# V as the stationary operand in a looped decode step, and 32 positions of K on TensorE in place of ScalarE's sums

## The chip, the cores and the metric

The kernel runs on one core of one Trainium2 chip. The metric is the time of one execution on the device in microseconds (us). TensorE's weight loads (PEld) and matmuls (PE), VectorE (DVE), ScalarE (ACT) and GpSimd (POOL) work beside each other; SyncE (SP) issues the large transfers. Each engine has its own list of instructions, read by its own sequencer, and engines wait for each other through semaphores. SBUF is the memory on the chip, with 128 partitions; PSUM is where TensorE writes.

## What is computed

One token for each of two batches passes through an attention block with a cache, and then through a gated MLP. The cache is what costs: 32 heads with 8192 positions of 128 numbers, for K and for V, in bf16, for two batches.

```python
def _A_ref(x, k_cache, v_cache, wq, wo):          # x: 2 x 1 x 512
    q = (x @ wq) ... 32 heads of 128
    scores = einsum("bhqd,bhkd->bhqk", q, k) * (Dh ** -0.5)
    p = softmax(scores, axis=-1)
    o = einsum("bhqk,bhkd->bhqd", p, v)
    return o ... @ wo

h = x + _A_ref(_layernorm(x), k_cache, v_cache, wq, wo)
h2 = h + _B_ref(_layernorm(h), W_gate, W_up, W_down)   # relu(gate) * up, then W_down
```

## The kernel before

The attention runs in 16 steps, `steps`, of one batch and four heads each (`H4`). A step's K is one block of 128 partitions by 256 positions (`NT`) by 128 numbers, 8 MiB; its V is another. In the block, 32 partitions (`QP`) belong to one head, so each partition holds 256 positions of one head. There are three block buffers, `buf`. K of step i goes to buffer (i-2) mod 3, and V of step i goes into the same buffer as soon as that K has been used up (`k_at`, `v_at`). So K of step i+1 can come in only when the V of step i-2 has been read.

`scores(i)` makes the 256 scores of a partition, for the positions in three ways:

- VectorE multiplies K by q in place (`mult`, L341) for `nmul` positions, 240 in most steps.
- The first 48 of these (`NACT`) are summed over their 128 numbers by ScalarE, one position at a time (`sum_up`, L348: one activation and one read of the accumulator each). The other 192 are added up by VectorE in four halving steps (L412) and one reduction (L416).
- The last 16 positions (`NPE`; 32 in the last step, none in the first) aren't multiplied: TensorE transposes them in chunks of eight (L356), ScalarE copies a chunk from PSUM to `kT` (L362), and TensorE multiplies the chunk by q (L364). ScalarE copies the results into the scores (L375).

`best(i)` takes the maximum of a partition (L312) and spreads it by a matmul (L314). `powers(i)` finds the step's maximum (L323), and ScalarE makes the four sets of exponentials into `pgz`, with their sums in `zc` (L326).

`values(i)` multiplies the exponentials with V on TensorE, in two forms. In the first 13 steps (`COLS`) the exponentials are stationary: a group of four positions (`T4`) with 16 columns is loaded as weights, and 512 numbers of V stream past, into a PSUM tile `po`. The first two groups are written out (L427); the other 62 are a loop on TensorE alone, `Fori`, with two groups a turn (`LOOP`), so 31 turns (L451 for the turn's own bookkeeping, L453 for the matmuls), whose addresses are worked out in registers from the turn's number w. A turn's records name these operations: FUSED_REGOPS and ALU_OP are register instructions, COMPARE_BRANCH ends the turn. The loop stands in a critical section: TensorE's sequencer waits for several semaphores on entry (L447, L659) and marks its end (L447). Because every head's exponentials meet every position's V there, the wanted parts are picked out later: `collect` copies `po` to `ob` (L465), and `turn` multiplies `ob` with the 0/1 pattern `sel` for a group of steps (L474) and forms the sums with `sums` (L295). In the last three steps V is stationary, 128 numbers of one position at a time, and the four columns of exponentials of that position stream past (L439), all 256 written out with fixed addresses.

The order on TensorE, VectorE, ScalarE and SyncE is the order in which the code emits it (`manual_schedule`). In a middle step it is: VectorE multiplies 16 and then 176 positions; TensorE transposes two chunks; ScalarE sums the first 16 positions and copies the last `po`; the two chunks are copied and multiplied; `powers(i-1)`; `turn(i-2)`; `values(i-1)` on TensorE; SyncE issues K of step i+1; ScalarE copies the chunks' scores, VectorE multiplies the last 48 positions, ScalarE sums 32 more; VectorE adds up, and `best(i)`. After that SyncE issues V of step i. So on TensorE the loop over V of step i-1 stands behind the transposes of K of step i, and the maximum of step i behind that loop.

Of the kernel before, what the change touches and what calls it, by code (L numbers as in the profile page):

```python
# [7 lines left out]
ACT = mybir.ActivationFunctionType  # L8
ALU = mybir.AluOpType
# [14 lines left out]
def kernel(  # L24
# [21 lines left out]
    H4 = 4  # L46
# [70 lines left out]
    ob = consts.tile([P, T4 * Dh], f32)  # L117
    ident = consts.tile([P, P], bf16)
# [5 lines left out]
    pick = consts.tile([P, B, QP], bf16)  # L124
    sel = consts.tile([P, T4, 4, H4], f32)
    eps_col = consts.tile([P, 1], f32)
# [43 lines left out]
    with tc.manual_schedule(engines=ORDERED):  # L170
# [13 lines left out]
        select(nscale, -SCALE, 0, [[-1, P]], 1)  # L184
        nc.gpsimd.memset(pgz, 0.0)
        nc.gpsimd.memset(zc, 0.0)
        nc.gpsimd.memset(ob, 0.0)

# [9 lines left out]

        nc.gpsimd.memset(sel, 0.0)
        for j in range(H4):  # L200
            select(sel[:, :, :, j], 1.0, -j, [[-H4, T4], [-32, 4]], 1)
        for k, n in enumerate(rows):
# [67 lines left out]

        groups = {3: (0, 0, 4), 7: (0, 4, 4), 11: (1, 0, 4)}
        for i in range(12, N):
            groups[i] = (1, i - NG, 1)
        assert NG == 8 and COLS == 13

        divided = {NG - 1: (0, 0, NG), N - 3: (1, 0, NG - 2), N - 2: groups[N - 2], N - 1: groups[N - 1]}
        o_ps = {}
        made = {}

        def group(i):  # L280
            e = min(k for k in groups if k >= i)
            return e, steps[i][1] - groups[e][1]

        waiting = []


        def o_of(i):
            key = B if i == N - 1 else steps[i][0]
            if key not in o_ps:
                o_ps[key] = ps2.tile([P, 2, Hq], f32, tag="o", name="o_ps")  # L290
            return o_ps[key]

        def sums(i):
            b, g0, n = groups[i]
            nc.tensor.matmul(  # L295
                out=o_of(i)[:, 1, H4 * g0:H4 * (g0 + n)], lhsT=mean_w, rhs=zc[:, b, g0:g0 + n, :], start=True, stop=True,
            )
# [21 lines left out]
        def powers(i):  # L319
            b, g = steps[i]  # L320
            scol = scols.pop(i)
            nm = small.tile([P, H4], f32, tag="nm")
            nc.vector.tensor_reduce(out=nm, in_=mx.pop(i), axis=AXIS.X, op=ALU.min)  # L323
            for j in range(H4):
                r = slice(j * QP, (j + 1) * QP)
                nc.scalar.activation(  # L326
                    out=_free(pgz[r, :], j, [[H4, NT]]), in_=scol[r, :], func=ACT.Exp, scale=SCALE,
                    bias=nm[r, j:j + 1], accum_out=zc[r, b, g, j:j + 1],
                )

        def scores(i):
# [3 lines left out]
            nmul = NT - NPE[i]  # L335
            na = NACT[i]
            scol = scols[i] = small.tile([P, NT], f32, tag=f"scol{i % 2}", name="scol")

            def mult(t0, t1):
# [3 lines left out]
                )  # L343

            def sum_up(t0, t1):
                for t in range(t0, t1):
                    whole = ps.tile([P, Dh], f32, tag="acc", name="whole")
                    nc.scalar.activation(  # L348
                        out=whole, in_=kt[:, t * Dh:(t + 1) * Dh], func=ACT.Copy, accum_out=scol[:, t:t + 1],
                    )  # L350

# [26 lines left out]
            if i == 0:  # L378
                for t0 in range(0, NT, NT // 4):
                    mult(t0, t0 + NT // 4)  # L380
                sum_up(0, na)
            elif last:
                mult(0, nmul)
                scores_of(by_columns([transposed(c0) for c0 in (0, TPC)]))
                sum_up(0, na)
# [21 lines left out]
            n = nmul - na  # L407
            width = Dh
            while width > 8:
                half = width // 2  # L410
                lo = _free(kt, na * Dh, [[Dh, n], [1, half]])
                nc.vector.tensor_tensor(  # L412
                    out=lo, in0=lo, in1=_free(kt, na * Dh + half, [[Dh, n], [1, half]]), op=ALU.add,
                )
                width = half
            nc.vector.tensor_reduce(  # L416
                out=scol[:, na:nmul], in_=_free(kt, na * Dh, [[Dh, n], [1, 8]]), axis=AXIS.X, op=ALU.add,
            )
# [4 lines left out]

        def products(i, u0, u1):
            v = buf[v_at[i]]
            for u in range(u0, u1):
                nc.tensor.matmul(  # L427
                    out=made[i][0:H4 * T4, :], lhsT=pgz[:, u * H4 * T4:(u + 1) * H4 * T4],
                    rhs=v[:, u * T4 * Dh:(u + 1) * T4 * Dh],
                    start=(u == 0), stop=(u == NT // T4 - 1), skip_group_check=True,  # L430
                )

        def values(i):
            v = buf[v_at[i]]
            if i >= COLS:
                sums(i)
                g = steps[i][1]
                for t in range(NT):
                    nc.tensor.matmul(  # L439
                        out=o_of(i)[:, 0, H4 * g:H4 * (g + 1)],  # L440
                        lhsT=v[:, t * Dh:(t + 1) * Dh], rhs=pgz[:, H4 * t:H4 * (t + 1)],
                        start=(t == 0), stop=(t == NT - 1),
                    )
                return

            made[i] = ps.tile([P, T4 * Dh], f32, tag="po", name="po")
            with tc.tile_critical(sync_engine=PE):  # L447
                products(i, 0, LOOP)

                at = {PE: LOOP_AT} if i == 0 else None  # L450
                with nc.Fori(1, NT // T4 // LOOP, 1, engines=[PE], head_slot=at) as w:  # L451
                    for u in range(LOOP):
                        nc.tensor.matmul(  # L453
                            out=made[i][0:H4 * T4, :],
                            lhsT=pgz[:, bass.ds((w * LOOP + u) * (H4 * T4), H4 * T4)],
                            rhs=v[:, bass.ds((w * LOOP + u) * (T4 * Dh), T4 * Dh)],
                            start=False, stop=True, skip_group_check=True,
                        )


        def collect(i):
            if i >= COLS:
                return
            _, k = group(i)
            nc.scalar.activation(  # L465
                out=ob[32 * k:32 * k + H4 * T4, :], in_=made.pop(i)[0:H4 * T4, :], func=ACT.Copy,
            )

        def turn(i):
            if i in groups:  # L470
                if i < COLS:
                    _, g0, n = groups[i]
                    for t in range(T4):
                        nc.tensor.matmul(  # L474
                            out=o_of(i)[:, 0, H4 * g0:H4 * (g0 + n)], lhsT=ob[:, t * Dh:(t + 1) * Dh],
                            rhs=sel[:, t, 0:n, :], start=(t == 0), stop=(t == T4 - 1),
                        )
                    sums(i)
                if i in divided:
                    waiting.append(i)  # L480

# [182 lines left out]
```

## Time and profile before

| what | before |
|---|---|
| median of three runs | 668.6 us (667.44 to 668.81) |
| the profiled execution | 667.49 us |
| its span, first to last instruction | 665.8 us |
| mean granted TensorE clock, share of full speed | 0.805 |
| VectorE busy | 507.8 us (76%) |
| ScalarE busy | 419.9 us (63%) |
| TensorE matmul busy | 366.8 us (55%) |
| read from memory | 281.05 MB |

The profile is of one execution. Its page gives the busy time of every engine, the span in 40 slices, the DMA queues, the chain of work that ended last, and the costliest groups of instructions by line of the kernel; "L453 PE" is the matmul of line 453. A q behind an engine (PEq, SPq, and PEldq in lists of a line's instructions) is its sequencer, whose instructions don't count as busy time. Times in lists are from the span's start. Rows of the list by time give start and length in us, engine, line, operation, operands, count, and in brackets how long the engine was idle before and what ended that.

### The profile page before, as it was taken

What the parts mean: (1) busy time and instruction counts of PE and PEld (TensorE: products, weight loads), DVE (VectorE), ACT (ScalarE), POOL (GpSimd) and SP (SyncE); (2) the same over time, 40 slices, a digit from 0 to 9 for tenths busy, and PEclk for the clock granted to TensorE, in tenths of its full rate; (3) what the DMA queues carried; (4) which work ended last, traced back from release to release, by engine and by line L of the source; (5) the groups of instructions that cost most, each with busy time, mean ns of one, the idle gap of its engine ahead of it and who ended that gap; (6) DMA issues with size and microseconds to landing.
All of it is one profiled execution on the core that took longest, in us unless ns stands there. A gap on an engine that the chain in (4) does not pass through costs nothing. (4 is left out here: it accounts for less than half of the span.)

```text
span 665.8 us, 10067 instructions
## 1 busy us (share of the span) xinstructions
PE 366.8 (55%) x2601; PEld 148.8 (22%) x2601; DVE 507.8 (76%) x192; ACT 419.9 (63%) x1766; POOL 8.4 (1%) x51
## 2 busy tenths in 40 slices
PE   2601574747647474664638657473865667543456
PEld 1201111111211221121112212111221131242456
DVE  0799969597795959879595996959689595987911
ACT  2596848487594848749475784848669465883720
POOL 5000000000000000000000000000000000000000
PEclk9955696988969798896978979698896979955555
DMA  8999999999999999999999999999999998999996
GB/s 369 448 441 441 434 441 406 426 437 434 441 437 438 434 433 418 433 434 434 437 438 429 425 426 429 423 409 437 426 433 418 425 407 367 429 443 439 414 416 260
DMA packets 6933, 281.45 MB, mean 423 GB/s; under 512 B 786, under 2 KB 884, under 8 KB 1524
## 3 DMA queue, kind: packets, MB, share of 16 engines
q1 hardware_dynamic: 6896, 281.06, 98.5%
q8 instruction: 15, 0.25, 0.1%
q14 instruction: 18, 0.15, 0.1%
q10 hardware_dynamic: 4, 0.00, 0.0%
HBM read 281.05 MB, written 0.00 MB: 422 GB/s over the span
## 5 line engine op out<-in xcount | busy, mean ns | idle before, releaser
L341 DVE TENSOR_TENSOR buf<-buf,qrep 128x2048 bf16<-128x2048 bf16 (+4 forms) x47 | 262.0, 5600 | 104.2 <-DMA buf<-in_A_k_cache_dram 104.2
L453 PE MATMUL po<-buf,pgz 128*16 x806 | 264.7, 408 | 87.8 <-issue 87.6
L348 ACT ACTIVATE whole<-buf 128x128 f32<-128x128 bf16 x752 | 211.4, 281 | 145.3 <-DVE buf L341 122.4
L412 DVE TENSOR_TENSOR buf<-buf 128x12288 bf16<-128x12288 bf16 (+3 forms) x64 | 203.1, 3173 | 2.2
L348 ACT ACTIVATION_READ_ACCUMULATOR whole<-buf 128x1 f32 x752 | 140.2, 186 | 0.2
L453 PEld LDWEIGHTS po<-buf,pgz 128*16 x806 | 72.5, 90 | 285.1 <-issue 241.6
L326 ACT ACTIVATE pgz<-scol,nm 32x256 bf16<-32x256 f32 x64 | 55.0, 859 | 14.0 <-DVE nm L323 10.4
L427 PE MATMUL po<-buf,pgz 128*16 128x512 bf16 x26 | 13.3, 614 | 85.4 <-ACT whole L348 83.0
L362 ACT ACTIVATE kT<-t_ps 128x1024 bf16<-128x1024 bf16 x32 | 32.8, 1024 | 18.9 <-PE t_ps L356 9.7
L439 PE MATMUL o_ps<-pgz,buf 128*128 128x4 bf16 x768 | 21.6, 166 | 20.5 <-DMA buf<-in_A_v_cache_dram 14.6
L364 PE MATMUL sc_ps<-qT,kT 128*128 128x4 bf16 x256 | 11.5, 167 | 38.1 <-ACT kT L362 38.1
L416 DVE TENSOR_REDUCE scol<-buf 128x192 f32<-128x1536 bf16 (+1 forms) x16 | 28.2, 1761 | 0.6
L314 PE MATMUL mx_ps<-nscale,pm 128*128 128x128 f32 x32 | 8.3, 345 | 34.0 <-DVE pm L312 29.3
L439 PEld LDWEIGHTS <-buf 128*128 128x128 bf16 x768 | 21.2, 104 | 21.0 <-DMA buf<-in_A_v_cache_dram 14.8
L356 PE MATMUL t_ps<-ident,buf 128*128 128x128 bf16 x256 | 19.6, 236 | 5.9 <-DMA buf<-in_A_k_cache_dram 5.9
L427 PEld LDWEIGHTS po<-buf,pgz 128*16 128x16 bf16 x26 | 1.3, 90 | 86.5 <-issue 86.5
L465 ACT ACTIVATE ob<-po 16x512 f32<-16x512 f32 x13 | 7.6, 587 | 18.2 <-PEq L447 18.2
L356 PEld LDWEIGHTS <-buf 128*128 128x128 bf16 x256 | 17.7, 107 | 6.4 <-DMA buf<-in_A_k_cache_dram 6.2
L364 PEld LDWEIGHTS <-kT 128*128 128x128 bf16 x256 | 8.7, 98 | 42.7 <-ACT kT L362 42.7
L326 ACT ACTIVATION_READ_ACCUMULATOR pgz<-scol,nm 32x1 f32 x64 | 15.9, 249 | 0.0
L314 PEld LDWEIGHTS mx_ps<-nscale,pm 128*128 128x128 f32 x32 | 5.4, 210 | 38.0 <-issue 28.3
L312 DVE TENSOR_REDUCE pm<-scol 128x1 f32<-128x256 f32 x16 | 6.7, 420 | 8.7 <-ACT whole L348 8.4
(88 smaller groups left out, 103.1 us busy)
## 6 DMA issues: line engine op xcount, KB each, us to landing
buf<-in_A_k_cache_dram SPq DMA_DIRECT2D x4, 2048.0 KB, 23.7
buf<-in_A_v_cache_dram SPq DMA_DIRECT2D x2, 4096.0 KB, 41.1
buf<-in_A_wq_dram SPq DMA_DIRECT2D x1, 4096.0 KB, 12.6
buf<-in_A_wo_dram SPq DMA_DIRECT2D x1, 2048.0 KB, 14.6
buf<-in_A_wo_dram SPq DMA_DIRECT2D x2, 1024.0 KB, 18.7
buf<-in_B_W_gate_dram SPq DMA_DIRECT2D x1, 1376.0 KB
buf<-in_B_W_up_dram SPq DMA_DIRECT2D x1, 1376.0 KB, 24.5
buf<-in_B_W_down_dram SPq DMA_DIRECT2D x1, 768.0 KB, 25.9
```

The costliest lines, as they stand in the source:

```text
L314: nc.tensor.matmul(out=mx[i].rearrange("p a b -> p (a b)"), lhsT=_free(pm, 0, [[0, P]]), rhs=nscale, start=True, stop=True,)
L326: nc.scalar.activation(out=_free(pgz[r, :], j, [[H4, NT]]), in_=scol[r, :], func=ACT.Exp, scale=SCALE, bias=nm[r, j:j + 1], accum_out=zc[r ...
L341: nc.vector.tensor_tensor(out=kv, in0=kv, in1=_free(qrep[b], g * Dh, [[0, t1 - t0], [1, Dh]]), op=ALU.mult,)
L348: nc.scalar.activation(out=whole, in_=kt[:, t * Dh:(t + 1) * Dh], func=ACT.Copy, accum_out=scol[:, t:t + 1],)
L356: nc.tensor.transpose(t_ps[:, k, :], kt[:, t * Dh:(t + 1) * Dh], ident)
L362: nc.scalar.activation(out=kT, in_=t_ps.pop(0).rearrange("p t s -> p (t s)"), func=ACT.Copy)
L364: nc.tensor.matmul(out=sc_ps[:, c0 + t, :], lhsT=kT[:, t * P:(t + 1) * P], rhs=_free(qT, H4 * g * B + b, [[B, H4]]), start=True, stop=True,)
L412: nc.vector.tensor_tensor(out=lo, in0=lo, in1=_free(kt, na * Dh + half, [[Dh, n], [1, half]]), op=ALU.add,)
L416: nc.vector.tensor_reduce(out=scol[:, na:nmul], in_=_free(kt, na * Dh, [[Dh, n], [1, 8]]), axis=AXIS.X, op=ALU.add,)
L427: nc.tensor.matmul(out=made[i][0:H4 * T4, :], lhsT=pgz[:, u * H4 * T4:(u + 1) * H4 * T4], rhs=v[:, u * T4 * Dh:(u + 1) * T4 * Dh], start=( ...
L439: nc.tensor.matmul(out=o_of(i)[:, 0, H4 * g:H4 * (g + 1)], lhsT=v[:, t * Dh:(t + 1) * Dh], rhs=pgz[:, H4 * t:H4 * (t + 1)], start=(t == 0) ...
L453: nc.tensor.matmul(out=made[i][0:H4 * T4, :], lhsT=pgz[:, bass.ds((w * LOOP + u) * (H4 * T4), H4 * T4)], rhs=v[:, bass.ds((w * LOOP + u) * ...
```

## The change

The 13 looped steps take V as the stationary operand too: the same form as the last three steps, one position at a time, 128 numbers of V loaded as weights and four columns of exponentials streaming past. Eight positions (`LOOP = 8`) are written out, and the other 248 are a loop of 31 turns with eight positions each, whose addresses come from registers. The results go straight to the step's columns of `o_ps`, so `po`, `ob`, `sel`, `collect`, `made`, `groups` and the matmuls with `sel` go, and `sums(i)` stands at the head of each `values(i)`.

On the K side `sum_up` goes. VectorE adds up all that it multiplies. TensorE takes 32 positions (24 in the first step, 48 in the second, 40 in the last), so VectorE multiplies and adds 224, in pieces of 176 and 48 where it was 16, 176 and 48. `pgz` has two buffers, for even and odd steps. In step 1 `powers(0)` stands ahead of the first multiplication.

```diff
-    FIRST = 16
     MIDDLE = 176
-    T4 = 4
...
-    LOOP = 2
+    LOOP = 8
...
-    pgz = consts.tile([P, NT * H4], bf16)
+    pgz = [consts.tile([P, NT * H4], bf16, name=f"pgz{s}") for s in range(2)]
...
-    NACT = {i: 32 if i == N - 1 else 48 for i in range(N)}
-    NPE = {i: 0 if i == 0 else 32 if i == N - 1 else 16 for i in range(N)}
+    NPE = {i: (24, 48)[i] if i < 2 else 40 if i == N - 1 else 32 for i in range(N)}
...
             else:
-                mult(0, FIRST)
                 if i == 1:
                     powers(i - 1)
-                mult(FIRST, FIRST + MIDDLE)
+                mult(0, MIDDLE)
                 t_ps = [transposed(c0) for c0 in (0, TPC)]
-                sum_up(0, FIRST)
-                if i >= 2:
-                    collect(i - 2)
                 sc_ps = by_columns(t_ps)
...
-                mult(FIRST + MIDDLE, nmul)
-                sum_up(FIRST, na)
+                mult(MIDDLE, nmul)
...
         def values(i):
+            b, g = steps[i]
             v = buf[v_at[i]]
+            p = pgz[i % 2]
+            o = o_of(i)[:, 0, H4 * g:H4 * (g + 1)]
+            sums(i)
+
+            def products(n):
+                for t in range(n):
+                    nc.tensor.matmul(
+                        out=o, lhsT=v[:, t * Dh:(t + 1) * Dh], rhs=p[:, H4 * t:H4 * (t + 1)],
+                        start=(t == 0), stop=(t == NT - 1), skip_group_check=True,
+                    )
+
             if i >= COLS:
-                sums(i)
...
+                products(NT)
                 return
 
-            made[i] = ps.tile([P, T4 * Dh], f32, tag="po", name="po")
             with tc.tile_critical(sync_engine=PE):
-                products(i, 0, LOOP)
+                products(LOOP)
 
                 at = {PE: LOOP_AT} if i == 0 else None
-                with nc.Fori(1, NT // T4 // LOOP, 1, engines=[PE], head_slot=at) as w:
+                with nc.Fori(1, NT // LOOP, 1, engines=[PE], head_slot=at) as w:
+                    vw = v[:, bass.ds(w * (LOOP * Dh), LOOP * Dh)]
+                    pw = p[:, bass.ds(w * (LOOP * H4), LOOP * H4)]
                     for u in range(LOOP):
                         nc.tensor.matmul(
-                            out=made[i][0:H4 * T4, :],
-                            lhsT=pgz[:, bass.ds((w * LOOP + u) * (H4 * T4), H4 * T4)],
-                            rhs=v[:, bass.ds((w * LOOP + u) * (T4 * Dh), T4 * Dh)],
+                            out=o, lhsT=vw[:, u * Dh:(u + 1) * Dh], rhs=pw[:, u * H4:(u + 1) * H4],
                             start=False, stop=True, skip_group_check=True,
                         )
```

More of the change, by code (lines that the diff above doesn't have):

```diff
@@ L114 @@
     qrep = [consts.tile([P, NG, Dh], bf16, name=f"qrep{b}") for b in range(B)]
-    pgz = consts.tile([P, NT * H4], bf16)
+    pgz = [consts.tile([P, NT * H4], bf16, name=f"pgz{s}") for s in range(2)]
     zc = consts.tile([P, B, NG, H4], f32)
-    ob = consts.tile([P, T4 * Dh], f32)
     ident = consts.tile([P, P], bf16)
@@ L124 @@
     pick = consts.tile([P, B, QP], bf16)
-    sel = consts.tile([P, T4, 4, H4], f32)
     eps_col = consts.tile([P, 1], f32)
@@ L184 @@
         select(nscale, -SCALE, 0, [[-1, P]], 1)
-        nc.gpsimd.memset(pgz, 0.0)
+        for t in pgz:
+            nc.gpsimd.memset(t, 0.0)
         nc.gpsimd.memset(zc, 0.0)
-        nc.gpsimd.memset(ob, 0.0)
         nc.gpsimd.memset(fold, 0.0)
@@ L197 @@
         select(quarter, 0.0, P // KC - 1, [[P // KC, KC]], -1, ALU.is_ge)
-        nc.gpsimd.memset(sel, 0.0)
-        for j in range(H4):
-            select(sel[:, :, :, j], 1.0, -j, [[-H4, T4], [-32, 4]], 1)
         for k, n in enumerate(rows):
@@ L268 @@
         nc.scalar.activation(out=qT, in_=qT_ps, func=ACT.Copy)
-        groups = {3: (0, 0, 4), 7: (0, 4, 4), 11: (1, 0, 4)}
-        for i in range(12, N):
-            groups[i] = (1, i - NG, 1)
         assert NG == 8 and COLS == 13
-        divided = {NG - 1: (0, 0, NG), N - 3: (1, 0, NG - 2), N - 2: groups[N - 2], N - 1: groups[N - 1]}
+        divided = {NG - 1: (0, 0, NG), N - 3: (1, 0, NG - 2), N - 2: (1, NG - 2, 1), N - 1: (1, NG - 1, 1)}
         o_ps = {}
[L278 to L282, printed above, removed]
         waiting = []
@@ L293, in sums @@
         def sums(i):
-            b, g0, n = groups[i]
+            b, g = steps[i]
             nc.tensor.matmul(
-                out=o_of(i)[:, 1, H4 * g0:H4 * (g0 + n)], lhsT=mean_w, rhs=zc[:, b, g0:g0 + n, :], start=True, stop=True,
+                out=o_of(i)[:, 1, H4 * g:H4 * (g + 1)], lhsT=mean_w, rhs=zc[:, b, g, :], start=True, stop=True,
             )
@@ L326, in powers @@
                 nc.scalar.activation(
-                    out=_free(pgz[r, :], j, [[H4, NT]]), in_=scol[r, :], func=ACT.Exp, scale=SCALE,
+                    out=_free(pgz[i % 2][r, :], j, [[H4, NT]]), in_=scol[r, :], func=ACT.Exp, scale=SCALE,
                     bias=nm[r, j:j + 1], accum_out=zc[r, b, g, j:j + 1],
@@ L335, in scores @@
             nmul = NT - NPE[i]
-            na = NACT[i]
             scol = scols[i] = small.tile([P, NT], f32, tag=f"scol{i % 2}", name="scol")
@@ L343, in mult @@
                 )
[L345 to L350, printed above, removed]
             def transposed(c0):
@@ L379, in scores @@
                 for t0 in range(0, NT, NT // 4):
-                    mult(t0, t0 + NT // 4)
-                sum_up(0, na)
+                    mult(t0, min(t0 + NT // 4, nmul))
+                scores_of(by_columns([transposed(c0) for c0 in (0, TPC)]))
             elif last:
@@ L410, in scores @@
                 half = width // 2
-                lo = _free(kt, na * Dh, [[Dh, n], [1, half]])
+                lo = _free(kt, 0, [[Dh, nmul], [1, half]])
                 nc.vector.tensor_tensor(
-                    out=lo, in0=lo, in1=_free(kt, na * Dh + half, [[Dh, n], [1, half]]), op=ALU.add,
+                    out=lo, in0=lo, in1=_free(kt, half, [[Dh, nmul], [1, half]]), op=ALU.add,
                 )
@@ L416, in scores @@
             nc.vector.tensor_reduce(
-                out=scol[:, na:nmul], in_=_free(kt, na * Dh, [[Dh, n], [1, 8]]), axis=AXIS.X, op=ALU.add,
+                out=scol[:, 0:nmul], in_=_free(kt, 0, [[Dh, nmul], [1, 8]]), axis=AXIS.X, op=ALU.add,
             )
@@ L422, in scores, with values @@
             best(i)
-        def products(i, u0, u1):
+        def values(i):
+            b, g = steps[i]
             v = buf[v_at[i]]
[L426 to L434, printed above, removed]
-            if i >= COLS:
-                sums(i)
[L437 to L443, printed above, removed]
+            p = pgz[i % 2]
[7 more added lines that the diff above has]
+                    )
+            if i >= COLS:
+                products(NT)
@@ L452, in values @@
                     for u in range(LOOP):
                         nc.tensor.matmul(
-                            out=made[i][0:H4 * T4, :],
-                            lhsT=pgz[:, bass.ds((w * LOOP + u) * (H4 * T4), H4 * T4)],
-                            rhs=v[:, bass.ds((w * LOOP + u) * (T4 * Dh), T4 * Dh)],
+                            out=o, lhsT=vw[:, u * Dh:(u + 1) * Dh], rhs=pw[:, u * H4:(u + 1) * H4],
                             start=False, stop=True, skip_group_check=True,
                         )
[L461 to L467, printed above, removed]
@@ L469, in turn @@
-        def turn(i):
[L470 to L480, printed above, removed]
+        def turn(i):
+            if i in divided:
+                waiting.append(i)
```

2 lines of the change are left out of this document (removed).

## The prediction

> **What bounds the kernel now.** I read the page's slices and queues first, then what the DMA queue itself waits for, then its issues in order of time.
>
> ```profile
> span 665.8 us, 10067 instructions
> DMA  8999999999999999999999999999999998999996
> q1 hardware_dynamic: 6896, 281.06, 98.5%
> SPq L145 <- DVE scol L416: 330.8, 15, 31.1
> SPq L145 <- PEq L447: 216.1, 13, 20.8
> 280.02 0.33 SPq L145 DMA_DIRECT2D buf<-in_A_v_cache_dram  x1
> 287.90 13.03 DVE L341 TENSOR_TENSOR buf<-buf,qrep 128x2048 bf16<-128x2048 bf16 x2 [7.46 <-DMA buf<-in_A_k_cache_dram]
> 297.39 0.33 SPq L145 DMA_DIRECT2D buf<-in_A_k_cache_dram  x1
> ```
>
> The DMA row is full in nearly every slice, and the queue that carries K and V is busy 98.5% of the span: the kernel streams 281 MB and the engines keep up. SP issues a V when VectorE has reduced the K that lies in its buffer (L416), and a K when the loop over V has left its block (L447). The last three rows show how early. A V is issued at 280.02 while the K ahead of it lands at 287.9; the next K is issued at 297.39, and that V lands only at 307.9, when TensorE's wait ahead of its loop ends. So both issues come 8 to 10 us before the queue would run dry. The issues of K from 101.83 to 493.77 are ten steps apart: 39.2 us a step, the time of 16.8 MB.
>
> How near is TensorE to that? Its own chain of a step is the loop over V, then the maximum (L314), the transposes of the next K, copy and matmul by ScalarE and TensorE in turn, the four exponentials, and the loop again. In the step from 537 to 573 that chain ran without a wait for a transfer: last turn at 537.22, first static matmul of the next loop at 545.73, last turn at 573.07, so 35.9 us. Spare: about 3 us of 39.2. This is the row to watch.
>
> **The loop, which decides.** These are the instructions of the present loop, sequencer's own included (count: shortest/median/longest ns):
>
> ```profile
> L451 PEldq FUSED_REGOPS  x403: 78/78/83, 74.2 to 572.5; - x135
> L451 PEldq ALU_OP  x403: 32/32/32, 74.7 to 573.0; - x135
> L451 PEldq COMPARE_BRANCH  x404: 76/208/225, 73.9 to 573.1; - x135
> L453 PEldq FUSED_REGOPS  x806: 42/58/79, 74.3 to 572.7; - x162
> L453 PEldq ALU_OP  x403: 36/36/42, 74.6 to 572.9; - x135
> 583.54 4.03 PE L439 MATMUL o_ps<-pgz,buf 128*128 128x4 bf16 x145 [1.94 <-DMA buf<-in_A_v_cache_dram]
> ```
>
> 403 turns are 13 loops of 31. A turn has two matmuls, and for them five register instructions and a branch: fused 78, fused 42, [load, matmul], fused 74, ALU 36, [load, matmul], ALU 32, branch 208. In the trace the next one starts 58 to 61 ns after the end of the one before, and 78 to 81 where a load and a matmul stand between. Sum: 78+59+42+78+74+59+36+81+32+61+208+58 = 866 ns. From branch to branch the loops turn every 884 to 890 ns (one loop, from 505.5 on, every 1034): 27.4 us for 31 turns. So the loop is paced by TensorE's sequencer; its two matmuls fill 0.63 us of a turn.
>
> The last row is the V-stationary form with fixed addresses: 145 pairs in 4.03 us, 27.8 ns each. The data of the new form is nearly free, but only while no register instruction stands between two pairs.
>
> The changed loop has eight positions a turn, so sixteen addresses that change with w. The product with w is shared, then every position adds its own constant to both. I take one fused instruction of 74 ns per position after the first, for this reason: the second position of today's turn (sum, products, both bases) needs 74 and 36, and a shared product removes about what the 36 did. Turn: first position 78+59+36+80 = 253, seven more of 74+79 = 1071, the end 32+61+208+58 = 359: 1683 ns. 31 turns: **52.2 us**, for 27.4 now. Bounds: the shortest fused row, 42, gives 1459 ns and 45.2 us; two register instructions per position (74+59+36+80 = 249 each) give 2355 ns and 73.0 us. I take 74 because this row adds for two addresses, as the new positions must.
>
> [...]
>
> **The rest of TensorE's chain**, from a loop's end to the next loop's first turn. End to transposes 0.8 (573.15 to 573.98), and 0.3 for a slower clock, since the array will be idle for most of the loop. Step 15 already has four chunks of eight positions, at that clock:
>
> ```profile
> 602.89 1.89 PE L356 MATMUL t_ps<-ident,buf 128*128 128x128 bf16 x16 [5.86 <-DMA buf<-in_A_k_cache_dram]
> 608.89 1.02 ACT L362 ACTIVATE kT<-t_ps 128x1024 bf16<-128x1024 bf16 x1 [0.52 <-PE sc_ps L364]
> 544.46 0.25 ACT L326 ACTIVATION_READ_ACCUMULATOR pgz<-scol,nm 32x1 f32 x1
> 545.73 0.59 PE L427 MATMUL po<-buf,pgz 128*16 128x512 bf16 x1 [2.34 <-PEq L447]
> ```
>
> Transposes to the end of the fourth copy: 602.89 to 609.91, 7.0 us (two chunks took 3.2). Four exponentials 3.5. Their end to the first static matmul, 544.71 to 545.73, 1.0: the critical section's waits; the new sums(i) lies beside it. Eight static pairs and the first register move 0.3. Together 12.9. The second pgz buys nothing: the exponentials stand behind the four copies on ScalarE, and these wait for transposes that stand behind the loop. So a step of TensorE takes 52.2+12.9 = **65.1 us against 39.2 for its transfers**: TensorE becomes the bound, by 26 us a step.
>
> **What else changes, and why it costs nothing then.** ScalarE loses 48 sums a step, 48 times 0.43 = 21 us, and one collect of 0.59, and gets two copies of 1.02; it waited 122 us for VectorE. VectorE multiplies 224 for 240 positions (16.5 to 15.2 us) and adds 224 for 192 (12.7 to 14.9, and the reduction 1.75 to 2.04): 1.2 us more, 32 of 65. Without the longer loop this would go into its wait of 104.2 us for K, 6 to 7 a step. The products with sel and their groups go (L474, 4.5 us in all). GpSimd's fills lie in the first 9 us. K i+1 and V i are issued as before, after the loop and after L416, by SP in the same order, with nothing moved past another; both land far ahead of need.
>
> **The sum.** First turn 74.2 as now, since V 0 lands at 72.7 either way: 74.3. Twelve steps of 65.1 and one loop of 52.2: loop 12 ends at 907.7 (573.15 now). Then K 15 goes out; V 14 waits for VectorE: 1.6 to the new minimum, 3.35 multiply, 14.9 adds, 2.0 reduction, so issue 22.0 later and landing 22 after that on an empty queue: 951.7. From V 14's landing on, the tail is today's: 622.9 to 665.8, 42.9. Span 994.6. One loop of thirteen now pays 150 ns more a turn in a gap between two instructions; a body of 27 instructions for 11 makes such a place likelier, so two loops at 4.7: 1004. The execution is 667.49 for a span of 665.8, so 1.7 more: **1006 us**. That execution stands 0.2% below the median of 668.6.
>
> **Rivals.**
> - *One register step for the turn, none per position* (not slower). Turn 253+7x21+359 = 759 ns, loop 23.5, step 36.4, under 39.2: the transfers stay the bound and the time is today's, 667 to 669, or a little less where ScalarE's sums ended last (8.4 us of VectorE's waits). It decides from a loop of 26.3 us, 850 ns a turn. For it: 27.8 ns a pair with fixed addresses. Against it: every pair of L453 has register instructions of its own today. [...]
> - *Cheaper addresses*, 42 ns: step 58.1, end 905 (74.3+697.2+45.2+86.9+1.7).
> - *Two instructions per position*: step 85.9, end 1267.
> - *The change not doing what it says*: the diff gives 32 positions to thirteen of the steps and 24, 48 and 40 at the ends; that moves 3 us at most.
>
> **How the numbers follow.** Forecast 0.75, cheaper addresses 0.08, two instructions 0.08, not slower 0.05, something else slower (fetch gaps in most loops, 31x0.15x13 = 60 us more) 0.04. The forecast's own terms, a turn of 1.65 to 1.80 us, 12 to 14.5 around it, up to four loops with a gap, give 970 to 1085. With the cheaper addresses the range is 900 to 1090. A measurement here can tell 0.2% from no change: faster 0.02, same 0.03, slower 0.95.
>
> **What would show it.** Right: L447's waits gone from TensorE's entry, SP waiting for PEq at almost every K, DMA near 6 tenths, turns of about 1.7 us with seven fused instructions of 74 more, steps of 65 us. Wrong: a turn under 0.85 us, or fewer register instructions than positions.

## The result and the profile after

The changed kernel takes **1017.1 us**, the median of three runs (1016.94 to 1021.14), against 668.6 before: 1.524 times as long, with a 95% interval of 1.519 to 1.529. Its profiled execution has a span of 1015.2 us, where the prediction's sum came to 1004, and a mean granted TensorE clock of 0.518.

The first lines are from its page: the span, the granted clock and the DMA share in 40 slices, and the queue that carries K and V.

```profile
span 1015.2 us, 16654 instructions
...
PEclk9555555555555555555555555555555555555555
DMA  9999296492771945909649268194590960954998
...
q1 hardware_dynamic: 6896, 281.06, 65.9%
```

The same 281.06 MB move, but the DMA row is no longer full. It swings between 0 and 9, because transfers now come in bursts with pauses between them. What SP waits for before it issues one (us in all, times, the longest) says who makes the pauses:

```profile
SPq L140 <- PEq L409: 581.4, 13, 52.0
SPq L140 <- DVE scol L383: 326.5, 15, 31.1
```

The 13 waits for the end of TensorE's critical section (L447 before, L409 now) have grown from 216.1 to 581.4 us. VectorE's part of the waits has not grown (330.8 before). Next the waits of ScalarE and VectorE, and of the array itself:

```profile
ACT kT L336 <- PE t_ps L330: 744.8, 14, 63.7
DVE nm L305 <- PE mx_ps L296: 420.5, 16, 39.4
PEld o_ps L417 <- issue: 205.2, 409, 0.9
...
DVE buf L322 <- DMA buf<-in_A_k_cache_dram: 27.7, 15, 5.9
...
PE mx_ps L296 <- PEq L409: 5.3, 13, 0.4
```

ScalarE and VectorE wait for TensorE, and hardly for data any more (27.7 us, where VectorE waited 104.2 for K). TensorE itself waits for "issue", which is time in which the engine waited for nothing that the profile shows: its own sequencer had not reached the next instruction. This is the loop by its instructions (count: shortest/median/longest ns, first and last start), in two lists, one for the line of the matmuls and one for the turn's bookkeeping:

```profile
L417 PEld LDWEIGHTS o_ps<-pgz,buf x3224: 101/104/106, 74.4 to 927.0; 128*128 x190
L417 PE MATMUL o_ps<-pgz,buf x3224: 164/184/188, 74.4 to 927.0; 128*128 x190
L417 PEldq FUSED_REGOPS  x2821: 74/74/74, 74.5 to 926.8; - x189
L417 PEldq ALU_OP  x403: 36/36/42, 74.3 to 925.8; - x135
```

```profile
L413 PEldq COMPARE_BRANCH  x404: 76/208/222, 74.0 to 927.1; - x135
L413 PEldq FUSED_REGOPS  x403: 78/78/83, 74.2 to 925.7; - x135
L413 PEldq ALU_OP  x403: 32/32/32, 75.6 to 927.0; - x135
```

3224 pairs of load and matmul are 403 turns of eight. Their 2821 fused instructions are seven a turn, one for every position after the first, and each lasts 74 ns. From branch to branch a turn takes 1.70 us (before: 0.884 for the same share of V). One step of TensorE in order of time, from the last turns of a loop to the second turn of the next:

```profile
455.85 0.97 PE L417 MATMUL o_ps<-pgz,buf 128*128 x6
457.21 0.76 PE L296 MATMUL mx_ps<-nscale,pm 128*128 128x128 f32 x2 [0.39 <-PEq L409]
457.76 1.91 PE L330 MATMUL t_ps<-ident,buf 128*128 128x128 bf16 x16
...
464.64 0.37 PE L338 MATMUL sc_ps<-qT,kT 128*128 128x4 bf16 x8 [1.18 <-ACT kT L336]
468.17 0.59 PE L277 MATMUL o_ps<-zc,mean_w 128*128 128x4 f32 x2 [3.15 <-ACT pgz L308]
469.79 0.38 PE L400 MATMUL o_ps<-pgz,buf 128*128 128x4 bf16 x8 [1.03 <-DVE buf L379]
470.13 1.34 PE L417 MATMUL o_ps<-pgz,buf 128*128 x8
471.90 1.28 PE L417 MATMUL o_ps<-pgz,buf 128*128 x8 [0.43 <-issue]
```

No row here waits for a transfer. Between the loop's end at 456.8 and the first pair of the next loop at 470.1 lie 13.3 us (13.1 to that loop's first register instruction); all the rest of a step is loop. The wait at 469.79 is put down to VectorE, one of whose adds happens to end within it. But the sequencer's own records fill the wait without a stop: from 468.80 on it runs the entry of the critical section, six semaphore instructions and a branch, 0.98 us to the first load, the same as in the kernel before (544.74 to 545.73). SP's issues in the same stretch:

```profile
457.18 0.33 SPq L140 DMA_DIRECT2D buf<-in_A_k_cache_dram  x1
478.45 0.33 SPq L140 DMA_DIRECT2D buf<-in_A_v_cache_dram  x1
522.97 0.33 SPq L140 DMA_DIRECT2D buf<-in_A_k_cache_dram  x1
```

K goes out at 457.18 and at 522.97: 65.8 us a step, for 16.8 MB that need 39.2. The last loop ends 354.0 us later than before (927.2 and 573.1), and the tail from there takes 88.1 us where it took 92.6. But for rounding, these are the 349.4 us between the spans.

### The profile page after: what moved, and what is told of

It is laid out like the page before. It is cut to its first block, busy times and chain, and to the rows that moved or that the text cites. A ratio compares the mean times of both kernels' runs of the same rounds, so it can differ in the third digit from the quotient of the medians.

```text
span 1015.2 us, 16654 instructions
## 1 busy us (share of the span) xinstructions
PE 664.6 (65%) x5627; PEld 461.5 (45%) x5627; DVE 523.6 (52%) x178; ACT 145.4 (14%) x287; POOL 8.0 (1%) x46
## 3 DMA queue, kind: packets, MB, share of 16 engines
q1 hardware_dynamic: 6896, 281.06, 65.9%
## 5 line engine op out<-in xcount | busy, mean ns | idle before, releaser
L417 PE MATMUL o_ps<-pgz,buf 128*128 x3224 | 510.1, 182 | 182.9 <-issue 181.1
L417 PEld LDWEIGHTS o_ps<-pgz,buf 128*128 x3224 | 335.3, 104 | 357.4 <-issue 205.2
L322 DVE TENSOR_TENSOR buf<-buf,qrep 128x22528 bf16<-128x22528 bf16 (+5 forms) x33 | 242.8, 7361 | 27.8 <-DMA buf<-in_A_k_cache_dram 27.7
L379 DVE TENSOR_TENSOR buf<-buf 128x14336 bf16<-128x14336 bf16 (+7 forms) x64 | 233.1, 3642 | 2.2
L336 ACT ACTIVATE kT<-t_ps 128x1024 bf16<-128x1024 bf16 x66 | 67.5, 1023 | 771.0 <-PE t_ps L330 744.8
L330 PE MATMUL t_ps<-ident,buf 128*128 128x128 bf16 x528 | 64.2, 308 | 4.2 <-DMA buf<-in_A_k_cache_dram 4.2
L330 PEld LDWEIGHTS <-buf 128*128 128x128 bf16 x528 | 54.0, 143 | 5.2 <-DMA buf<-in_A_k_cache_dram 4.2
L338 PE MATMUL sc_ps<-qT,kT 128*128 128x4 bf16 x528 | 24.5, 168 | 41.4 <-ACT kT L336 41.4
L383 DVE TENSOR_REDUCE scol<-buf 128x224 f32<-128x1792 bf16 (+3 forms) x16 | 32.2, 2011 | 0.5
L400 PEld LDWEIGHTS <-buf 128*128 128x128 bf16 x768 | 21.4, 105 | 17.0 <-DMA buf<-in_A_v_cache_dram 9.5
L349 ACT ACTIVATE scol<-sc_ps 32x32 f32<-32x32 f32 (+3 forms) x64 | 12.1, 189 | 2.4 <-PE sc_ps L338 1.4
## 6 DMA issues: line engine op xcount, KB each, us to landing
buf<-in_A_wq_dram SPq DMA_DIRECT2D x1, 4096.0 KB, 12.9
```

Of the source, the lines that this page charges most:

```text
L322: nc.vector.tensor_tensor(out=kv, in0=kv, in1=_free(qrep[b], g * Dh, [[0, t1 - t0], [1, Dh]]), op=ALU.mult,)
L330: nc.tensor.transpose(t_ps[:, k, :], kt[:, t * Dh:(t + 1) * Dh], ident)
L336: nc.scalar.activation(out=kT, in_=t_ps.pop(0).rearrange("p t s -> p (t s)"), func=ACT.Copy)
L338: nc.tensor.matmul(out=sc_ps[:, c0 + t, :], lhsT=kT[:, t * P:(t + 1) * P], rhs=_free(qT, H4 * g * B + b, [[B, H4]]), start=True, stop=True,)
L349: nc.scalar.activation(out=scol[r, nmul:NT], in_=sc_ps[r, :, j], func=ACT.Copy)
L379: nc.vector.tensor_tensor(out=lo, in0=lo, in1=_free(kt, half, [[Dh, nmul], [1, half]]), op=ALU.add,)
```

## The experiments

The theory: TensorE's loop is the whole loss, and in it the register instructions that make each position's addresses, run one after the other by TensorE's sequencer. Its rivals: **A**, the array, whose small matmuls at a clock of 0.5 are slow in themselves; **B**, the turn's counter and branch; **C**, the changed K side (transposes, copies and longer adds ahead of the maximum); **D**, the loop as such (its body's place, its fetch), whatever instructions are in it. The kernel before, measured beside each series, took 668.0 to 668.5 us. Where no interval is given, a time is that of a single execution.

### Both addresses fixed

```diff
-                    vw = v[:, bass.ds(w * (LOOP * Dh), LOOP * Dh)]
-                    pw = p[:, bass.ds(w * (LOOP * H4), LOOP * H4)]
+                    vw = v[:, 0:LOOP * Dh]
+                    pw = p[:, 0:LOOP * H4]
```

> The changed kernel, but the eight positions in the loop's body have fixed addresses (positions 0 to 7 in every turn), so that a turn has no register instruction but its counter; the output leaves out the other 248 positions of V in the 13 looped steps. Theory (the loop is paced by one register instruction of 74 ns per position): a turn is eight pairs at 21 to 28 ns, counter 32, branch 208 and the gaps, 0.53 to 0.60 us; the loop 17 to 19 us; a step of TensorE 30 to 32, under the transfers' 39.2; time 664 to 672. Rival A (loading V as weights and the 184 ns matmuls themselves fill the loop, at a TensorE clock of 0.5): the loop stays near 53 us and the time above 1000. Rival B (the loop's counter and branch): the same 53 us, since both remain.

Measured: 662.3 us, beside 668.4 for the kernel before, and 2 us below the range expected. The lists of the loop's lines, and what SP still waits for at the end of the critical section:

```profile
L417 PEld LDWEIGHTS o_ps<-pgz,buf x3224: 102/104/118, 74.1 to 551.7; 128*128 128x128 bf16 x190
L417 PE MATMUL o_ps<-pgz,buf x3224: 166/166/188, 74.1 to 551.8; 128*128 128x4 bf16 x190
```

```profile
L413 PEldq COMPARE_BRANCH  x404: 76/208/340, 73.9 to 551.7; - x135
L413 PEldq ALU_OP  x403: 36/36/42, 74.2 to 551.6; - x135
```

```profile
SPq L140 <- PEq L409: 5.0, 14, 0.7
```

The same 3224 pairs run in the same 403 turns with the same branch of 208 ns; the fused instructions are gone, and with them the loss. A turn takes 388 to 399 ns on average, less than expected: its median of 383 is the counter, the branch and the gaps behind them (36+61+208+78), so the eight pairs lie beside these. A and B fall. The mean granted clock was 0.528, where the changed kernel had 0.518, so the low clock costs nothing here. SP's waits for the end of the critical section have shrunk from 581.4 us to 5.0, and the transfers are the bound again.

### One of the two addresses fixed

```diff
-                    pw = p[:, bass.ds(w * (LOOP * H4), LOOP * H4)]
+                    pw = p[:, 0:LOOP * H4]
```

> The changed kernel, but only the address of V follows the turn; the exponentials are those of positions 0 to 7 in every turn (their product with the right V is left out). Half the address work. Theory: the register instruction of a position gets shorter, from 74 to about 50 ns (between the fused rows of 42 and 74 that the traces show), and none goes away: 128 ns a position for 152, a turn 1.42 us for 1.70, 8.9 us less in each of 13 loops, 116 in all: 885 to 905. Rival A (the array's loads and matmuls, at half clock): 1010 to 1020, since every load and matmul stays.

Measured: 891.6 us, a turn of 1.41 us. The register instructions of the positions:

```profile
L417 PEldq FUSED_REGOPS  x2821: 46/46/46, 74.2 to 801.4; - x189
```

As many fused instructions as in the changed kernel, each 28 ns shorter: it adds for one address and not for two. Seven a turn are 0.20 of the 0.29 us by which a turn is shorter. The rest is the turn's first position, which makes one address as well: its ALU_OP of 36 ns is gone, with the gap of 59 behind the instruction ahead of it (that none would go was a miss). So the step from 1017 to 892 follows in the main the length of the positions' instructions, and the rest of the way to 662 their existence.

### The address work doubled

```diff
-                    vw = v[:, bass.ds(w * (LOOP * Dh), LOOP * Dh)]
-                    pw = p[:, bass.ds(w * (LOOP * H4), LOOP * H4)]
+                    at_w = w * LOOP
...
-                            out=o, lhsT=vw[:, u * Dh:(u + 1) * Dh], rhs=pw[:, u * H4:(u + 1) * H4],
+                            out=o, lhsT=v[:, bass.ds((at_w + u) * Dh, Dh)], rhs=p[:, bass.ds((at_w + u) * H4, H4)],
```

> The changed kernel with each address written out as (8 w + u) times the width, as the loop of before has it, so that the sum with u is a register operation of its own; the same result. Theory: a second register instruction per position, of 36 ns and a gap of 59 to 61, 96 ns more for seven of eight positions, a turn 2.36 to 2.40 us, 21 us more in each loop: 1280 to 1305. Rival A (the array): no change, 1010 to 1020.

Measured: 1284.7 us, a turn of 2.39 us:

```profile
L416 PEldq FUSED_REGOPS  x3224: 42/74/79, 74.4 to 1193.2; - x190
...
L416 PEldq ALU_OP  x2821: 32/32/42, 74.6 to 1193.3; - x189
```

A second register instruction of 32 ns per position costs 0.69 us a turn (2.39 less 1.70), so 98 ns for each of seven: its own 32, a gap of 59, and a few ns more at the other instructions. This is also the prediction's rival of two instructions per position, priced there at 1267.

### Thirty-two positions a turn

```diff
-    LOOP = 8
+    LOOP = 32
```

> The changed kernel with 32 positions a turn in place of eight: 7 turns of a loop and 32 positions ahead of it; the same result. Theory: a position goes on costing 152 ns, the rest of a turn 637 less 152; a turn 5.3 to 5.4 us, the loop 37.5, a step 14.6 shorter: 810 to 835. Rival B (the counter and the branch of a turn are the cost): seven turns of their 0.36 us in place of 31 are 8.6 us less, but then the positions would cost next to nothing and the time would fall to the transfers' 665. Rival D (a body of some 100 instructions can't be kept near the sequencer): a turn several us longer than the sum, above 900.

Measured: 826.6 us; a turn takes 5.46 to 5.51 us (5.72 in the first loop), a little over what was expected. By the shortest, each further position costs (5.46 - 1.70) / 24 = 156 ns, about as much as in a turn of eight (74 and a gap of 78 to 79). A quarter of the counters and branches doesn't make the position cheaper. The kernel is faster for two plain reasons: the end of a turn comes seven times a step instead of 31, and 32 positions instead of eight are written out ahead of the loop. B falls once more. D would have to put a price on each position, at any length of the body, and falls as far as the main loss goes.

### All 256 positions written out

```diff
-            if i >= COLS:
+            if i >= 0:
```

> The changed kernel with all 256 positions of every step written out with fixed addresses, no loop; the same result. Theory: 256 pairs at 27.8 ns are 7.1 us, and with stops for the instructions' own fetch as in the last three steps before (2.5 us, one or two per step) 10 to 13; a step of TensorE is then 23 to 26, the transfers bound again, and the time is 662 to 672. Rival A (the array itself): above 1000. A second doubt: 13 steps of 512 instructions more to fetch beside the transfers could stop TensorE for longer than in the last steps; from 14 us of stops per step on the time would rise.

Measured: 667.0 us (666.79 to 667.22), a ratio to the kernel before of 0.998, 0.9971 to 0.9989. The new form of the products and the new K side together cost nothing when no address is made in a register. The matmuls of all 16 steps, what the array waited for ahead of them (us in all, times, the longest), and the queue that carries instructions (packets, MB):

```profile
L400 PE MATMUL o_ps<-pgz,buf x4096: 166/166/188, 72.6 to 647.2; 128*128 128x4 bf16 x196
```

```profile
PE o_ps L400 <- DMA buf<-in_A_v_cache_dram: 55.4, 15, 10.2
PE o_ps L400 <- issue: 46.1, 16, 3.9
```

```profile
q8 instruction: 44, 0.72, 0.4%
```

It waits for V again. It also stops 16 times, once a step, for 2.9 us on average. The waits name no cause, but the trace's DMA records point to one: each of the 16 stops ends 1.2 to 1.6 us after the end of a packet of 16 KiB on the instruction queue (the first, from 77.95 to 80.64, after one from 78.13 to 79.20). By these times they can be waits for instructions, as the expectation had them, but no run took the packets away; beside transfers of 39 us a step they are hidden (667.0 us in all).

### The K part alone, and the V part alone

The K part in the kernel before:

```diff
-    NACT = {i: 32 if i == N - 1 else 48 for i in range(N)}
-    NPE = {i: 0 if i == 0 else 32 if i == N - 1 else 16 for i in range(N)}
+    NACT = {i: 0 for i in range(N)}
+    NPE = {i: 0 if i == 0 else 40 if i == N - 1 else 32 for i in range(N)}
...
-                sum_up(0, FIRST)
```

> The kernel before, with its loop over V unchanged, but 32 positions of K by TensorE (40 in the last step, none in the first) and none summed by ScalarE. Theory: TensorE's chain of a step goes from 35.9 to 39.0 us by two chunks of 1.53, just under the transfers' 39.2; time 667 to 680, which is 0 to 12 us of the 349 that the whole change costs. Rival C (the K side carries the loss: VectorE adds 17% more, ScalarE's sums had been free): 32 us of VectorE in a step would have to end last; above 700.

The V part, which is the changed kernel with the K side of before put back:

```diff
-    NPE = {i: (24, 48)[i] if i < 2 else 40 if i == N - 1 else 32 for i in range(N)}
+    FIRST = 16
+    NACT = {i: 32 if i == N - 1 else 48 for i in range(N)}
+    NPE = {i: 0 if i == 0 else 32 if i == N - 1 else 16 for i in range(N)}
...
-                mult(0, MIDDLE)
+                mult(0, FIRST)
+                mult(FIRST, FIRST + MIDDLE)
...
+                sum_up(0, FIRST)
...
+                sum_up(FIRST, na)
```

> The changed kernel's loop over V (eight positions a turn, V stationary) with the K side of before: 16 positions by TensorE, 48 summed by ScalarE. Theory: a step of TensorE is 65.7 less two chunks of 1.53, 62.6 us; ScalarE's sums lie beside the loop; time 974 to 982, and a turn stays at 1.70 us. Rival C (the K side carries the loss): below 800.

Measured: the K part alone 663.6 us (663.28 to 664.39), a ratio of 0.993, 0.9914 to 0.9942; the V part alone 969.6 us, some 4 below the range expected. So C falls: the K side is no loss, and the kernel with it alone is even a little faster, as long as the transfers are the bound. The expectation for it (no change or a loss) was a miss, taken up at the end. In the V part alone a turn takes 1.70 us as in the whole change, and a step 62.6 us, 3.1 less than the changed kernel's 65.7. This is what the two further chunks of transposes and copies cost where TensorE is the bound: a change that is free, or better, in one bound costs 3.1 us a step in the other. Between 13 loops lie 12 such steps. Their 37.2 us and the changed kernel's 11.3 us of slow turns (below; the V part alone has none), taken from its 1015.2, give 966.7; the span was 967.8. The expectation had left out the slow turns.

### Another place for the loop

The loop's body is put at a chosen place in TensorE's list of instructions (`LOOP_AT`, 169 in both kernels). In the changed kernel one loop turned much slower than the others (and two a little: 1.74 and 1.78 us a turn). First the branches of the loop before it, then its own:

```profile
L413 PEldq COMPARE_BRANCH  x31: 76/207/208, 736.5 to 787.7; - x31
```

```profile
L413 PEldq COMPARE_BRANCH  x31: 76/208/217, 802.5 to 861.4; - x31
```

30 turns in 51.1 us (from the starts before rounding), and 30 in 58.9: 1.70 and 1.96 us a turn. The instructions last as long; one gap, the one behind the turn's first register instruction, is about 310 ns instead of 59. The kernel before has such a loop as well, the second of these two:

```profile
L451 PEldq COMPARE_BRANCH  x31: 76/208/208, 546.5 to 573.1; - x31
```

```profile
L451 PEldq COMPARE_BRANCH  x31: 76/208/208, 506.2 to 537.2; - x31
```

0.885 and 1.034 us a turn. Here it is the gap behind the second register instruction, 242 ns instead of 78. The edit, in the changed kernel and then in the kernel before with 155, 60 and 100:

```diff
-    LOOP_AT = 169
+    LOOP_AT = 139
```

> The changed kernel with the head of its first loop at slot 139 of a block of instructions in place of 169, and so all loops 30 instructions earlier in their blocks; nothing else. In the changed kernel the loop of step 11 takes 1963 ns a turn where most take 1704, 260 of it in one gap after its first instruction. Theory (the gap hangs on where the loop's body lies): the turn of that loop falls to 1704 and the time by 7.8 us to 1007 to 1011, or another loop takes the gap over and the time stays. Rival (the gap hangs on what is computed or transferred in that step): loop 11 keeps its 1963.

Measured: 1008.1 us (1007.1 to 1012.75), a ratio to the kernel before of 1.510, 1.506 to 1.515; every loop turns in 1.70 to 1.71 us. So 9 of the 349 us belong to the place of the loop, and not to its work.

> The kernel before with the head of its first loop at slot 155 in place of 169; nothing else. Its loop of step 11 takes 1034 ns a turn where the others take 884 to 890, 4.6 us in all, and the K that is issued at its end comes 4 us late for the transfers. Theory: that loop falls to 884 as well, and the time by 3 to 5 us, to 663 to 665: what 32 positions of K by TensorE alone gave (663.6) was then this and not the K side. Rival (the K side gave it): the time stays at 668.

> The kernel before with the head of its first loop at slot 60; nothing else. At slot 169 one loop of 13 (step 11) turns every 1034 ns in place of 884, at slot 155 two (steps 1 and 6) do, and the time was 1.1 us less. Which loop is met is not known ahead. If no loop is met, the theory that the K side gave nothing expects 663 to 665, the time of the K part alone (no loop met there); the rival, that TensorE's 32 positions and the freed ScalarE gave most of it, expects 666 to 668 even then. If a loop is met, its step says how much a late or an early one costs.

> The same with slot 100, for a second place of the loops: with no loop met 663 to 665 by the theory that only the gap in a loop separates before from the K part alone, 666 to 668 by the rival that the K side does.

Measured, each with its ratio to the kernel before: 667.1 us at 155 (0.998, 0.9972 to 0.9990), 667.0 at 60 (0.998, 0.9970 to 0.9988), 667.4 at 100 (0.998, 0.9975 to 0.9993). The gap went from the loop where it was to others: two slow loops at 155 and at 100, one at 60, all at 1.03 to 1.04 us a turn. A slow loop delays one K by some 4.6 us, and the next step makes 3.4 of that good: at 60, K issues lay 43.8 us apart and then 35.9, where 39.2 is the mean. So, by an estimate from these issues, a slow loop costs about 1 us and not 5; the rest is the transfers' slack at work. No place that was tried for the kernel before was free of slow loops, so what it would take without any wasn't measured, and whether the K side gains by itself was not put to the test.

What makes a place slow can be read from the traces. Count TensorE's instructions on from the slot of the first loop, each loop's body once and each load with its matmul. In the kernel before, the body is 10 instructions long, and the slow loops start at 254 of 256, counted from 0 (slot 169), at 253 and 247 (155), at 249 (60), at 254 and 247 (100): each lies across a multiple of 256. In the changed kernel (27 instructions) the three slow loops start at 240, 248 and 255, with 1.74, 1.78 and 1.96 us a turn. In the twelve kernels here whose loops have bodies of up to 34 instructions, 14 of 156 loops lie across such a multiple, and these 14 are the slowest of their kernels, one by 7 ns a turn and the others by 17 or more. At slot 139, in both parts alone and with both addresses fixed no loop lies across one, and none is slow. In the kernel before, the stretched gap is where the multiple falls: at 254 and 253 around the first pair, at 249 around the second, at 247 right ahead of the branch. Why the crossing takes time turn after turn stays open.

### The K part with four groups a turn

The one combination that seemed to have something left: the K part, and the old form of the products with four groups a turn and their shared product.

```diff
-    LOOP = 2
-    LOOP_AT = 169
+    LOOP = 4
+    LOOP_AT = 166
...
+                    vw = v[:, bass.ds(w * (LOOP * T4 * Dh), LOOP * T4 * Dh)]
+                    pw = pgz[:, bass.ds(w * (LOOP * H4 * T4), LOOP * H4 * T4)]
...
-                            lhsT=pgz[:, bass.ds((w * LOOP + u) * (H4 * T4), H4 * T4)],
-                            rhs=v[:, bass.ds((w * LOOP + u) * (T4 * Dh), T4 * Dh)],
+                            lhsT=pw[:, u * H4 * T4:(u + 1) * H4 * T4],
+                            rhs=vw[:, u * T4 * Dh:(u + 1) * T4 * Dh],
```

with `NACT`, `NPE` and `sum_up` as in the K part alone.

> The kernel before with 32 positions of K by TensorE, none summed by ScalarE, and four groups of four positions a turn of its loop over V, their addresses formed from a product shared by the turn, at slot 166. Theory: 253 + 3 x 153 + 359 = 1071 ns of the sequencer for four groups where it was 1768; the loop is then bound by its 64 streams of 512 numbers, 20 us at full clock to 27 at half; TensorE's chain is 33 to 39 of the transfers' 39, so the transfers stay the bound and the time is 660 to 665, no more than 0.3% from the 663.6 of the K part alone.

Measured: 663.9 us (663.43 to 664.23), a ratio of 0.993, 0.9916 to 0.9943, the same as the K part alone. A turn of four groups takes 1.09 to 1.11 us (1.19 in one loop, which lies across a multiple of 256), where two turns of two take 1.77. So TensorE's loop is about 40% shorter, some 16 us where 20 to 27 were expected, and nothing comes of it: the transfers are the bound. The two kernels with the K part and the old products are the fastest found that compute the whole block, 0.7% under the kernel before.

## Why the prediction was right

The forecast was 1006, its range 900 to 1090; the time is 1017.1. The mechanism was the one forecast, and each term can be set beside its row.

- **What bounds.** Right: TensorE in place of the transfers, SP waiting for its sequencer at all 13 K, the DMA share at 0.61 from the first loop to the last. The fixed addresses and the written-out form show the cause by taking it away.
- **One fused instruction of 74 ns per position.** Right: seven a turn, 74 each, with the 78, 36, 32 and 208 around them as read from the old loop. The reason given for 74, that this row adds for two addresses, holds too: with one address the row is 46.
- **The loop.** A turn of 1.683 us was forecast, 1.704 measured. The old loop shows a like difference: its rows sum to 866 ns and it turned in 884. I saw that and didn't carry it over. In the trace it is one gap in most turns that lasts some 20 ns longer than its usual 58 to 81, and a different one from turn to turn; what stretches it stays open. A small error the other way: the last turn's branch falls through in 76 ns and not 208. Together a loop takes 52.66 us for 52.2, 6.0 in all 13. This is the largest mis-sized term.
- **The rest of a step.** 12.9 forecast, 13.1 measured, near only because its errors cancel. Loop to transposes 0.9 for 1.1, transposes to the last copy 6.8 for 7.0, exponentials 3.5 as said, the static pairs to the first register instruction 0.1 for 0.3. But from the exponentials to the first static matmul it took 1.7 us for 1.0: "the new sums(i) lies beside it" was wrong. sums(i) starts at 468.17, the entry of the critical section follows at 468.80, and the static pairs start at 469.79. The 0.3 for a slower clock has a reason that no run shows, the array's idle time. The granted clock was 0.50 from 74 to 927 us and 0.87 from 74 to 573 before, but PE was busy 69% of the one stretch and 61% of the other.
- **Loops with a gap.** Two at 4.7 us forecast, 9.4; measured one of 8.0, and two smaller ones of 2.2 and 1.1, 11.3 in all. That the sum comes near is luck: the gap cost 255 ns a turn in one loop, not 150, and far less in two others. That a longer body makes such places likelier fits the count of the place above: three loops of 13, and one before. That the gaps are fetches, as the forecast's chances call them, no run shows.
- **The tail.** 86.9 forecast, 88.1 measured.

The misses are 6.0 for the loops, 2.2 for the rest of twelve steps, 1.9 for the gaps and 1.2 for the tail, less 0.1 for the first turn: 11.2 us, by which the span lies above the sum.

Of the rivals, "no register step per position" names the point well: with the fixed addresses a step's loop took 12 us, far under its limit of 26.3, and the time went to 662. The diff just doesn't make that loop. For the K side the forecast had four copies at 7.0 us where two took 3.2, so 3.8 a step; the V part alone shows 3.1 where TensorE is the bound, and the K part alone none where the transfers are. The 3 us at most for other counts of positions in three steps were not taken apart by any run.

## What to carry to other kernels

Count what a looped engine's own sequencer must run for each small instruction: here 74 ns and a gap of some 80 for each register-addressed matmul, against 28 for a pair with fixed addresses, so that a form with cheap data and four times as many matmuls took half as much time again. Set that sum against the period of whatever bounds the kernel, and if it is over, put more data under each address (four positions at a time, as before), or write the addresses out. A cost or a gain that is hidden under one bound (the transposes, with 3.1 us a step; the shorter loop, with no gain) has to be priced again under the other.

## What was not expected of the hardware

- **The place of a loop's body** costs 150 ns a turn in one loop of the kernel before and 37 to 259 in three of the changed kernel, mostly in one gap of a turn, and it moves with the slot. By the count above it falls on the 14 of 156 loops whose body lies across a multiple of 256 instructions. The DMA records show no packet for every turn: the instruction queue (q8) moved none during the slow loops of the kernel before, at any of the four slots, and one during each of the changed kernel's three.
- **The long stretches of written-out pairs** stopped once a step for 2.9 us, 46.1 us in all, each time until 1.2 to 1.6 us after the end of a packet of the instruction queue.
- **The K part alone is 0.7% faster** than the kernel before, though both are bound by their transfers. One part is that it has no slow loop, worth about 1 us by the estimate above. The other 3 to 4 us stay open. From 200 to 500 us of each span (busy time and count of PE, PEld, DVE, ACT and POOL, clock, DMA share, GB/s), first the kernel before and then the K part alone:

```profile
200.00:500.00 300.00, 180.10 (x782) 59.98 (x782) 236.39 (x78) 195.60 (x826) 0.00 (x0) 0.87 1.00 430
```

```profile
200.00:500.00 300.00, 198.19 (x1040) 72.62 (x1040) 250.13 (x81) 67.08 (x125) 0.00 (x0) 0.88 1.00 433
```

With the queue full in both, it moves 433 GB/s and not 430 while ScalarE is busy a third as long. That the one causes the other was not shown; no run changed ScalarE's work alone.
